# Attention with sinks and a two-layer product: chunk 0 masked in PSUM, its first product begun pair by pair, and chunk 1 moved ahead

## The chip, the core and the metric

The kernel runs on one NeuronCore of a Trainium2 chip. The core has five engines that run their own instruction queues: TensorE (PE, matrix products into PSUM), VectorE (DVE), ScalarE (ACT), GpSimd (POOL, which here issues the loads that also cast from float32 to bf16) and SyncE (SP, which here issues the other DMAs). They meet through semaphores. Sixteen DMA engines carry the transfers of all queues. The metric is the device time of one execution in microseconds (us); less is better. In the listings q0 is the DMA queue that POOL feeds, q1 the one that SP and ACT feed.

## The reference, cut to what matters

```python
batch, n_heads, seq, head_dim = (4, 8, 768, 64)
n_sink, window = (4, 64)
is_retrieval = [1, 0, 1, 0, 0, 0, 1, 0]
# attention, per batch and head
scores = (q @ k.T) / sqrt(head_dim)
causal = rel >= 0                                  # rel = query position - key position
keep   = causal & (key_pos < n_sink | (rel < window))
mask   = causal if is_retrieval[head] else keep
a      = softmax(where(mask, scores, -1e9))
x      = a @ v                                     # heads side by side: (3072, 512)
# two products with a leaky ReLU between
h   = x @ w_in                                     # 512 -> 2048
g   = maximum(0.01 * h, h)
out = g @ w_out                                    # 2048 -> 512, float32
```

Inputs and output are float32. The heads with full causal attention (0, 2, 6) are called retrieval heads below, the other five stream heads.

## The kernel before, in words

The 3072 tokens (4 batches of 768) are cut into eight chunks of 384 (`CH`); chunk n is half c of batch b, `divmod(n, 2)`. The schedule is written out by hand: the order of the Python calls is the order of the instructions on each engine, and the semaphores follow from it. Each chunk passes through these steps.

- **Loads** (`load`, `load_w`). POOL issues q, k and v in three transfers of 128 tokens each, and each weight in four quarters. At most eight of POOL's transfers are under way, because each waits for the eighth one before it. Chunk 0's k comes through SP into a float32 tile (`load_k0`).
- **Preparation.** q and k are transposed so that the head dimension lies on the partitions. `prep_first` (chunk 0) and `prep_pair` (chunks 1 and 2, one pair of heads at a time) use PE transposes into PSUM, followed by copies on DVE or ACT into `qts[n]` and `kt[b % 2]`. Chunks 3 to 7 use DMA transposes on SP (`prep_dma`), out of the buffers `kz` and `qb`. `zeros` and `zeros_k` clear the halves that must be zero. `v_shift` makes `vb`, the values moved by 64 tokens, with two DMAs on SP; `v_shift_pe` makes it for chunk 0 with products and copies.
- **Attention** (`Attention`). Each unit has a score part `qk` (products into a PSUM bank, an exponential on ACT into `at` or `ats`, a mask multiplication on DVE) and a value part `do_av`, which follows `LAG` slots later. The value parts of a head pair accumulate in one bank `po`; `finish` adds the sink's part, takes the reciprocal of the last column (`linv`) and writes the scaled rows `xs`. `x_t` transposes `xs` on PE and ACT copies it to `xts[n]`. From chunk 4 on this is a DMA transpose instead. `slots` cuts the whole into slots, so that other work can be merged between them.
- **Product 1** (`in_slots`): sixteen tiles of 128 rows of h, each four products into one bank (`ph`, at L497) and one leaky ReLU on ACT into `gs[n]` (L499).
- **Product 2** (`out_slots`): three token tiles, each sixteen products of 512 columns (L510), cut into five or six slots; then a DVE copy to `o` and a store on SP.

Eight PSUM banks are shared by tag: `ph`, `psS` and `po` have two each, `py` and `pt` one. `merge` puts one list of slots evenly among another.

The order at the start is chunk 0's preparation, its attention `a0`, eight tiles of its product 1 (`in0[0:8]`), then chunk 1's preparation pair by pair among further tiles and the first scores of chunk 1's attention `a1`, the rest of `a1` among the rest of `in0` and half of `out0`, and then chunk 1's product 1 merged with the rest of `out0`. Between them POOL issues, in this order: q and v of chunk 0, w_in quarter 0, two small masks, w_in quarters 1 and 2, k, q and v of chunk 1, w_in quarter 3, w_out, then chunks 2 and 3. `warm_up` and the extra transposes in `x_t` are products whose result nobody reads; they keep PE running while it waits. From chunk 2 on a loop merges product 1 of chunk n, product 2 of chunk n - 1 and the attention of chunk n + 1.

Of the kernel before, what the change touches and what calls it, by code (L numbers as in the profile page):

```python
# [11 lines left out]
FP32 = mybir.dt.float32  # L12
# [9 lines left out]
def kernel(  # L22
# [119 lines left out]

    def mask_causal():
        nc.gpsimd.memset(m_caus[:], 1.0)
        keep(m_caus[:], [[1, 128]], ALU.is_ge, 0, -1)

    def masks():
        nc.gpsimd.memset(m_w[:], 1.0)
        keep(m_w[:], [[-1, 64]], ALU.is_gt, 0, 1)
        keep(m_w[:], [[1, 64]], ALU.is_ge, 64, -1)  # L150

        nc.gpsimd.memset(m_h[:], 1.0)
        keep(m_h[:], [[-NS, H]], ALU.is_ge, 0, 1)
        keep(m_h[:], [[NS, H]], ALU.is_ge, NS - 1, -1)
# [8 lines left out]

    def late_constants():
# [3 lines left out]
        for h in range(H):  # L168
            if IS_RETR[h]:
                nc.vector.memset(m_h[:, h : h + 1], 0.0)  # L170
# [28 lines left out]
    def v_shift_pe():  # L199

        w = 7 * (D + 1)
        for t in range(2):
# [5 lines left out]
            if t == 0:  # L208
                nc.scalar.activation(out=vb[0][:, t, 1:H, :], in_=src, func=ACTF.Copy)
            else:  # L210
                nc.vector.tensor_copy(vb[0][:, t, 1:H, :], src)
# [8 lines left out]
    def prep_pair(n, p, tag="pt", eng=("v", "v", "v")):  # L220
# [20 lines left out]
        move(eng[2], qts[n][:, p, :], pt[:, 1, 0:3, :])  # L241

# [17 lines left out]
    def prep_first():  # L260
# [36 lines left out]

        k_rows(0, 0)
        k_rows(0, 1)
        shifts()  # L300
        k_rows(1, 0, True)
        k_rows(1, 1)
        for h in range(H):
            sink_keys(0, h // 2, h % 2)
# [9 lines left out]
    class Attention:  # L314
# [37 lines left out]
        def retr(self, h):  # L352
# [5 lines left out]
            for grp in groups:  # L358
                box = {}

                def qk(grp=grp, box=box):
                    s = self.score()
                    a = rot.tile([128, CH], BF16, name="at", tag="at", bufs=6)
                    off = 0
                    for j, (kj, lo) in enumerate(grp):
# [5 lines left out]
                        off += w  # L371
                    nc.scalar.activation(out=a[:, 0:off], in_=s[:, 0:off], func=ACTF.Exp, scale=SM)  # L372
                    if len(grp) == 2:
# [18 lines left out]
        def stream(self, h):  # L392
# [4 lines left out]
            def qk():  # L397
# [3 lines left out]
                for m in range(6):  # L401
# [4 lines left out]
                        skip_group_check=True)  # L406
                av_ = a[:, :, 0:4:3, :]
                nc.scalar.activation(  # L408
                    out=av_, in_=s[:, 0:CH].rearrange("p (j e f) -> p j e f", j=3, e=2),
                    func=ACTF.Exp, scale=SM)  # L410
                if c == 0:
# [34 lines left out]
        def x_t(self, p, xs, tag="pt"):  # L446
            pt = bank(tag, [128, 2, 4, 128], BF16)
            for j in range((6, 4, 6, 10)[p] if self.n == 0 else 0):
# [3 lines left out]
            nc.scalar.activation(out=xts[self.n][:, p, :], in_=pt[:, 0, 0:3, :], func=ACTF.Copy)  # L452

        def slots(self, extra=(), order=range(H), extra_at=None, LAG=2, XLAG=3, sink_after=None):

            extra = list(extra)
# [9 lines left out]
            r, box = [], {}  # L466
# [102 lines left out]
    for i in range(4):  # L569
        load_w("out", i)  # L570
# [94 lines left out]
```

## Time and profile before

| | |
|---|---|
| device time, median of 4 runs | 244.95 us (244.54 to 245.69) |
| the profiled execution | 244.54 us, its span 242.8 us |
| granted PE clock | 1.00 throughout |
| start of the first score, of product 1 | 9.74 us, 19.47 us |
| start of product 1 of chunk 1, of chunk 2 | 49.46 us, 81.41 us |
| product 1 (L497) | 492 matmuls recorded, 326 ns each |
| product 2 (L510, banks py) | 238 recorded, 371 ns each |
| loads by POOL (q0) | 13.24 MB as written, 74.4% of 16 engines |
| other DMA (q1) | 16.95 MB, 35.6% of 16 engines |

The span runs from the first to the last recorded instruction. A matmul's recorded length includes the time in the pipeline, so that lengths of neighbours overlap; the distance between two starts is what PE gives to one. The shares of the DMA queues are the time that their packets took, and those of two queues overlap. A row of the timeline gives the start, the length, the engine and line, the operation with target and source, how often it comes in a row, and in brackets how long the engine was idle before it and what released it.

### The profile page before, as it was taken

The page shows a single profiled execution, that of the slowest core. Times are in us where ns is not written, and L with a number is a line of the kernel's source. Part 1 is how long each engine was busy: PE and PEld are TensorE (multiplying, and loading weights), DVE is VectorE, ACT ScalarE, POOL GpSimd, SP SyncE. Part 2 cuts the span into 40 slices and gives each one's busy share as a digit, 9 for nine tenths or more (in the row PEclk, how much of TensorE's full clock was granted, in tenths as well). Part 3 has the DMA queues.
Part 4 walks back from the last instruction along what each step waited for, and adds up shares of the span by engine and source line. Part 5 has one row for each costly group of instructions (what it writes and reads, how often), then busy time and mean ns, then how long its engine had stood idle before and what let it go on. Part 6 is the DMA issues. An engine that isn't in the chain of part 4 may idle for free.

```text
span 242.8 us, 5110 instructions
## 1 busy us (share of the span) xinstructions
PE 228.9 (94%) x2028; PEld 138.7 (57%) x2056; DVE 90.5 (37%) x261; ACT 131.5 (54%) x285; POOL 78.3 (32%) x106
## 2 busy tenths in 40 slices
PE   7989889899999999899997999999999999999994
PEld 2765546556665667466544566566556665455553
DVE  6898422616465234334410343234411352111121
ACT  2776688433753698656445664466447764333300
POOL 7976832788109863384450000000000000000000
PEclk9999999999999999999999999999999999999999
DMA  9999999999999999999999932377220211111112
GB/s 162 143 180 166 178 233 196 154 182 134 156 155 209 199 130 147 161 174 142 199 140 179 170 99 62 90 152 140 76 62 0 63 32 59 46 43 43 44 45 86
DMA packets 112779, 30.54 MB, mean 126 GB/s; under 512 B 103540, under 2 KB 108916, under 8 KB 112756
## 3 DMA queue, kind: packets, MB, share of 16 engines
q0 software_dynamic: 76224, 13.24, 74.4%
q1 hardware_dynamic: 36432, 16.95, 35.6%
q8 instruction: 16, 0.26, 0.5%
q14 instruction: 7, 0.06, 0.1%
q10 hardware_dynamic: 100, 0.02, 0.1%
HBM read 27.28 MB, written 6.29 MB: 138 GB/s over the span
## 4 chain that ended last, share of the span: by engine, by line
PE 78%; DMA 8%; POOL 6%; ACT 3%; DVE 3%; issue 2%; POOLq 0%
PE ph L497 29%; PE py L510 20%; PE po L334 6%; PE pt L510 6%; PE psS L367 5%; DMA qb<-in_q_dram 4%; PE psS L510 4%; DMA xt<-xs 3%; PE ph L510 3%; PE psS L403 2%; POOL qb L93 2%; PE psS L347 2%; DVE o L515 1%; POOL kb L93 1%; POOL va L93 1%
## 5 line engine op out<-in xcount | busy, mean ns | idle before, releaser
L497 PE MATMUL ph<-xt,w_in_bf 128*128 128x384 bf16 x492 | 100.0, 326 | 1.5 <-DMA xt<-xs 1.4
L499 ACT ACTIVATE g<-ph 128x384 bf16<-128x384 f32 x123 | 60.5, 492 | 59.0 <-PE ph L497 58.3
L510 PE MATMUL py<-w_out_bf,g 128*128 128x512 bf16 (+1 forms) x238 | 63.4, 371 | 2.1 <-DVE o L515 0.6
L497 PEld LDWEIGHTS <-w_in_bf 128*128 128x128 bf16 x512 | 45.8, 97 | 29.5 <-issue 0.5
L510 PEld LDWEIGHTS <-g 128*128 128x128 bf16 x400 | 36.0, 97 | 28.9 <-issue 2.2
L372 ACT ACTIVATE at<-psS 128x384 bf16<-128x384 f32 x81 | 38.9, 491 | 12.7 <-PE psS L367 10.9
L93 POOL DMA_DIRECT2D qb<-in_q_dram x24 | 21.4, 902 | 21.7 <-DMA qt<-qb 10.6
L515 DVE COPY o<-py 128x512 f32<-128x512 f32 (+1 forms) x16 | 10.8, 674 | 45.3 <-PE py L510 45.0
L86 POOL DMA_DIRECT2D kz<-in_k_dram x30 | 22.5, 770 | 15.9 <-DMA kt<-kz 12.7
L367 PE MATMUL psS<-qt,kt 128*128 128x384 bf16 (+2 forms) x104 | 25.9, 290 | 1.3 <-ACT at L372 1.1
L93 POOL DMA_DIRECT2D va<-in_v_dram x24 | 21.2, 900 | 9.1 <-DMA w_in_bf<-in_moe_w_in_dram 3.1
L408 ACT ACTIVATE ats<-psS 128x384 bf16<-128x384 f32 x38 | 18.6, 493 | 5.2 <-PE psS L403 4.8
L334 PE MATMUL po<-va,at 128*128 128x65 bf16 x237 | 20.2, 194 | 0.3 <-DVE at L376 0.3
L334 PEld LDWEIGHTS <-at 128*128 128x128 bf16 x252 | 15.8, 98 | 7.4 <-DVE at L376 1.4
L440 DVE TENSOR_TENSOR xs<-po,linv 128x384 bf16<-128x384 f32 x30 | 16.7, 557 | 1.0
L378 DVE TENSOR_TENSOR at<-at,m_caus 128x128 bf16<-128x128 bf16 x24 | 5.4, 224 | 31.0 <-ACT at L372 31.0
L367 PEld LDWEIGHTS <-kt 128*128 128x128 bf16 x108 | 10.4, 98 | 10.4 <-issue 3.0
L510 PE MATMUL pt<-w_out_bf,g 128*128 128x512 bf16 x57 | 15.7, 379 | 0.4
L403 PEld LDWEIGHTS <-kt 128*128 128x128 bf16 x240 | 11.8, 98 | 5.5 <-issue 0.2
L334 PEld LDWEIGHTS <-ats 128*128 128x128 bf16 x240 | 11.6, 97 | 4.3 <-issue 0.8
L376 DVE TENSOR_TENSOR at<-at,m_caus 128x256 bf16<-128x256 bf16 x24 | 7.0, 292 | 16.1 <-ACT at L372 16.0
L403 PE MATMUL psS<-qt,kt 128*128 128x64 bf16 x228 | 12.8, 193 | 0.0
(115 smaller groups left out, 199.3 us busy)
## 6 DMA issues: line engine op xcount, KB each, us to landing
out_dram<-o SPq DMA_DIRECT2D x23, 256.0 KB, 3.0
qb<-in_q_dram POOLq DMA_DIRECT2D x24, 128.0 KB, 7.3
va<-in_v_dram POOLq DMA_DIRECT2D x24, 128.0 KB, 7.6
w_in_bf<-in_moe_w_in_dram POOLq DMA_DIRECT2D x4, 512.0 KB, 8.0
w_out_bf<-in_moe_w_out_dram POOLq DMA_DIRECT2D x4, 512.0 KB, 13.3
kz<-in_k_dram POOLq DMA_DIRECT2D x30, 64.0 KB, 7.9
vb<-va SPq DMA_DIRECT2D x8, 195.0 KB, 7.3
vb<-va SPq DMA_DIRECT2D x6, 130.0 KB, 5.9
```

The lines of the kernel that those rows point to most:

```text
L86: nc.gpsimd.dma_start(out=kz[n % 2][:, g, hh::2, D * hh : D * hh + D], in_=nat[nm][b, c, :, hh::2, g])
L93: nc.gpsimd.dma_start(out=o, in_=nat[nm][b, c, :, :, g])
L334: nc.tensor.matmul(o, lhsT=lhsT, rhs=rhs, start=first, stop=False, skip_group_check=True)
L367: nc.tensor.matmul(s[:, off : off + w], lhsT=kt[i][:, p, hh, 128 * kj : 128 * kj + 128], rhs=qts[n][:, p, lo:CH], start=(j == 0), stop=(j ...
L372: nc.scalar.activation(out=a[:, 0:off], in_=s[:, 0:off], func=ACTF.Exp, scale=SM)
L403: nc.tensor.matmul(s[:, 64 * m : 64 * m + 64], lhsT=kt[i][:, p, hh, k0 : k0 + 128], rhs=qts[n][:, p, 64 * m : 64 * m + 64], start=(m == 0) ...
L408: nc.scalar.activation(out=av_, in_=s[:, 0:CH].rearrange("p (j e f) -> p j e f", j=3, e=2), func=ACTF.Exp, scale=SM)
L440: nc.vector.tensor_tensor(xs[:], po[:, :, :, 0:D], linv.to_broadcast([128, 3, 2, D]), op=ALU.mult)
L497: nc.tensor.matmul(ph[:, 0:CH], lhsT=w_in_bf[:, g, 128 * t : 128 * t + 128], rhs=xts[n][:, g, :], start=(g == 0), stop=(g == KG - 1))
L499: nc.scalar.activation(out=gs[n][:, t, :], in_=ph[:, 0:CH], func=ACTF.Prelu, alpha=0.01)
L510: nc.tensor.matmul(py[n][:, 0 : c1 - c0], lhsT=gs[n][:, ng, 128 * tt : 128 * tt + 128], rhs=w_out_bf[:, ng, c0:c1], start=(ng == 0), stop= ...
L515: nc.vector.tensor_copy(o[:, 0 : c1 - c0], py[n][:, 0 : c1 - c0])
```

## The change

The masks of chunk 0 are no longer multiplied into the exponentials on DVE. Negative masks `n_caus` and `n_win0` (0 where a score is kept, -30000 where not) are added to the scores in PSUM by a product with the identity. `masks` builds them, `m_w` and `m_h` on DVE, in `prep_first`, ahead of the kt copies; POOL's masks go. The second of chunk 0's four kt copies moves from DVE to ACT, and one `vb` copy from ACT to DVE. DVE's clearing of `kt[0]` for chunk 1 moves into chunk 0's attention; that of `kz` moves to POOL.

The first four tiles of chunk 0's product 1 (`in_first`) are computed side by side in four banks, one head pair after another, between the `x_t` of the pairs. Then all of chunk 1 is prepared at once (`prep_two`, two head pairs in one bank, with larger copies). Chunk 1's k and q are loaded ahead of w_in quarter 1, and its v ahead of quarter 2. The value parts of chunk 1 follow their scores by ten slots at first, two at the end (`lag`), with thirteen `at` buffers. Product 1 of chunk 1 comes ahead of most of product 2 of chunk 0, whose first tile uses a bank of tag `psS`. `load(4)` and `prep_dma(3)` keep their places in the list of calls, while chunk 2's preparation comes later in it.

```diff
+    def negative(out, m):
+        nc.vector.tensor_scalar(out, m, NEG, -NEG, op0=ALU.mult, op1=ALU.add)
+
+    def masks():
+        with nc.allow_low_precision("one term of each sum is not zero"):
+            nc.vector.tensor_reduce(m_h[:], ident[:, 0 : NS * H].rearrange("p (h r) -> p h r", r=NS),
+                                    axis=mybir.AxisListType.X, op=ALU.add)
+        for h in range(H):
+            if IS_RETR[h]:
+                nc.vector.memset(m_h[:, h : h + 1], 0.0)
+        negative(n_caus[:], m_caus[:])
+        nc.vector.tensor_sub(m_w[:], m_caus[:, 64:128], m_caus[:, 0:64])
+        nc.vector.tensor_copy(n_win0[:, 0, :], n_caus[:, 0:64])
+        negative(n_win0[:, 1:], spread(m_w[:], 5, 64))
+        nc.vector.memset(n_win0[0:NS, 1, :], 0.0)
...
+    def prep_two(n, nm, half, tag, eng):
...
+        pt = bank(tag, [128, 2, 4, 128], BF16)
+        for e in range(2):
+            p = 2 * half + e
+            for g in range(3):
+                nc.tensor.transpose(pt[:, e, g, :], cast[nm, n][:, g, 2 * p : 2 * p + 2, :], ident[:])
...
+        if nm == "k":
+            for hh in range(2):
+                r = slice(64 * hh, 64 * hh + 64)
+                move(eng[hh], kt[b % 2][r, ps2, hh, CH * c : CH * c + CH], pt[r, :, 0:3, :])
+        else:
+            for e in range(2):
+                p2 = slice(2 * half + e, 2 * half + e + 1)
+                move(eng[e], qts[n][:, p2, :], pt[:, e : e + 1, 0:3, :])
...
+        masks()
         k_rows(0, 0)
-        k_rows(0, 1)
-        shifts()
+        k_rows(0, 1, True)
         k_rows(1, 0, True)
         k_rows(1, 1)
+        shifts()
...
-                    a = rot.tile([128, CH], BF16, name="at", tag="at", bufs=6)
+                    a = rot.tile([128, CH], BF16, name="at", tag="at", bufs=13)
...
+                    if n == 0:
+                        for o in (0,) if len(grp) == 1 else (0, 256):
+                            nc.tensor.matmul(s[:, o : o + 128], lhsT=ident[:], rhs=n_caus[:], start=False,
+                                             stop=True, skip_group_check=True)
...
+                if n == 0:
+                    nc.tensor.matmul(s[:, 0:CH], lhsT=ident[:], rhs=n_win0.rearrange("p m t -> p (m t)"),
+                                     start=False, stop=True, skip_group_check=True)
...
+    def in_first(n, tags):
+        phs = []
+        def step(g):
+            if g == 0:
+                phs.extend(in_bank(n, t, tag) for t, tag in enumerate(tags))
+            for t, ph in enumerate(phs):
+                in_part(n, t, ph, g)
+                if g == KG - 1:
+                    leaky(n, t, ph)
+        return [lambda g=g: step(g) for g in range(KG)]
...
     load_w("in", 0)
-    masks()
+    load(1, "kq")
     load_w("in", 1)
+    load(1, "v")
     load_w("in", 2)
-    load(1)
     load_w("in", 3)
...
+    for t in kz:
+        nc.gpsimd.memset(t[:, :, 0::2, D:], 0.0)
+        nc.gpsimd.memset(t[:, :, 1::2, 0:D], 0.0)
     prep_first()
-    a0 = Attention(0, ("psS", "ph"), po_tags=("po", "po", "py", "po"),
-                   x_tags=("pt", "ph", "psS", "pt")).slots(order=[0, 2, 1, 3, 4, 5, 6, 7], LAG=4, XLAG=3, sink_after={0, 2})
-    warm_up(12)
+    A0 = Attention(0, ("psS", "ph"), po_tags=("po", "po", "py", "po"))
+    a0 = A0.slots(order=[0, 2, 1, 3, 4, 5, 6, 7], lag=lambda t: 4, XLAG=None, sink_after={0, 2})
+    warm_up(8)
     run(a0[0:4])
-    late_constants()
-    run(a0[4:6])
     sink_values(0)
+    zeros(0, 1)
+    run(a0[4:6])
     v_shift_pe()
-    run(a0[6:])
-    zeros(0, 1)
-    nc.vector.memset(ksink[1][:], 0.0)
-    zeros(1, 0)
-    zeros_k(1)
-    zeros_k(0)
+    run(a0[6:15])
+    i0 = in_first(0, ("ph", "psS", "ph", "psS"))
+    A0.x_t(0, "pt", 4)
+    run(a0[15:])
+    A0.x_t(1, "po", 6)
+    run(i0[0:1])
+    A0.x_t(2, "pt")
+    run(i0[1:2])
+    A0.x_t(3, "py")
+    run(i0[2:4])
+    in0 = in_slots(0, ("ph",))
+    prep_two(1, "k", 0, "py", "vs")
+    prep_two(1, "k", 1, "pt", "vs")
+    prep_two(1, "q", 0, "py", "sv")
+    prep_two(1, "q", 1, "pt", "sv")
     load(2)
     load(3)
-    in0 = in_slots(0, ("ph", "psS"))
-    run(in0[0:8])
...
+    A1 = Attention(1, po_tags=("po", "po", "po", "pt"), x_tags=("py",))
+    a1 = A1.slots(order=[0, 2, 6, 1, 3, 4, 5, 7], lag=lambda t: max(2, 10 - t // 2))
+    run(a1[0:4])
     v_shift(1, nc.sync)
-    run(a1[3:6])
-    run(merge(in0[11:], a1[6:14]))
-    out0 = out_slots(0, ("py", "py", "py"))
-    run(merge(out0[0:8], a1[14:] + [lambda: None] * 6))
+    run(merge(in0[4:8], a1[4:10]), a1[10:14])
+    run(merge(in0[8:12], a1[14:20]))
+    out0 = out_slots(0, ("psS", "ph", "py"))
+    run(merge(in0[12:16] + out0[0:3], a1[20:]))
+    late_constants()
+    nc.vector.memset(ksink[1][:], 0.0)
+    zeros(1, 0)
     v_shift(2, nc.sync)
     load(4)
+    in1 = in_slots(1)
+    run(in1[0:12], merge(in1[12:], out0[3:5]))
     run(prep_dma(3))
-    x = merge(in_slots(1), out0[8:])
-    run(x[:8])
     a2 = [lambda j=j: prep_pair(2, j, ("pt", "psS")[j % 2]) for j in range(4)] + Attention(2).slots()
-    run(merge(x[8:] + out_slots(1, ("ph", "py", "ph")), a2))
+    run(merge(out0[5:] + out_slots(1, ("ph", "py", "ph")), a2))
```

## The prediction

> **What bounds the kernel now.** I read the page's rows by slice first, then the windows, then the timelines of the first 50 us engine by engine, then the waits of POOL and of the tile xt. TensorE (PE) has the work:
>
> ```profile
> PE 228.9 (94%) x2028; PEld 138.7 (57%) x2056; DVE 90.5 (37%) x261; ACT 131.5 (54%) x285; POOL 78.3 (32%) x106
> PEclk9999999999999999999999999999999999999999
> DMA  9999999999999999999999932377220211111112
> ```
>
> The clock is full throughout, and the DMA engines are taken until slice 23 (140 us). Busy PE overstates work, since a row's length contains the pipeline. I count work by the spacing of starts: a product-1 tile (four matmuls, L497) 0.65 us, an L510 matmul 0.216, an L367 score 0.162, a stream head's six L403 matmuls 0.18, a value matmul of L334 0.03, a transpose 0.055. The windows then divide the run:
>
> ```profile
> 24.92:49.46 24.54, 21.38 (x231) 13.61 (x232) 9.42 (x28) 16.62 (x39) 13.71 (x17) 1.00 1.78 190
> 49.46:81.41 31.95, 31.69 (x268) 19.09 (x272) 14.39 (x42) 14.77 (x32) 19.43 (x25) 1.00 1.70 169
> ```
>
> From 49.46 to 81.41 the work is 31.8 us (product 1 of chunk 1 10.4, 71 L510 matmuls 15.3, preparation and attention of chunk 2 6.1): nothing is lost. From 24.92 to 49.46 it is 19.3 us (24 transposes 1.3, eight product-1 tiles 5.2, attention of chunk 1 7.35, 25 L510 matmuls 5.4), so **5.2 us are lost**. Before 22 us PE waits on chains of copies. Hence only the start, the stage of chunk 1, and the few late waits on DMA can give anything.
>
> **1. Start of chunk 0.**
>
> ```profile
> 8.88 0.81 ACT L306 ACTIVATE qt<-po 128x768 bf16<-128x768 bf16 x1 [0.77 <-PE po L281]
> 9.74 0.32 PE L367 MATMUL ph<-qt,kt 128*128 128x384 bf16 x1
> 19.47 1.06 PE L497 MATMUL ph<-xt,w_in_bf 128*128 128x384 bf16 x4
> ```
>
> ScalarE (ACT) waits for the transposed q, copies it, and the first score follows at 9.74; product 1 starts at 19.47. The change puts the new masks on VectorE (DVE) after the cast that ends at 5.67 and ahead of the first kt copy. A reduction to 128x8 and a multiply-add do not occur in this trace. By neighbours (L438 0.19, L161 0.17, L165 0.31, the three L170 memsets 0.13) they make 1.3 us together; bounds 0.9 and 1.9. The kt copy could not start before 6.28 anyway, so it moves to 7.0 and lasts to 7.95 (L292, 0.97). The second kt copy goes to ACT. In the order of instructions it waits for DVE's copy out of the same bank, though the two read different partitions. *The row* nearest is an ACT copy of bank py that sat 1.74 us behind DVE's:
>
> ```profile
> 27.34 0.49 ACT L235 ACTIVATE qt<-py 128x384 bf16<-128x384 bf16 x1 [1.74 <-DVE kt L233]
> ```
>
> *The rule* is that of the Trainium skill, page "PSUM — Partial Sum Buffer", section "PSUM bank collisions raise a hardware error": access need be kept apart only by bank and 32-partition quadrant. Rows 0-63 and 64-127 are different quadrants, so by the rule ACT starts at 6.3 and the first score stays at 9.74. By the row ACT does 7.95 + 0.80 + 0.80 + 0.81 = 10.35, first score 10.4: **0.7 later**. I take the row, because the order names the wait; no run here shows the rule's case.
>
> DVE goes on in a line: kt copy after ACT's (9.55 to 10.5), shifts 0.25, ksink 0.76, second q half 0.56 (ends 12.1, was 10.89), sink values 0.7, two kt memsets moved here at 0.9 each, two vb copies 1.1: 15.8 us. In the old trace the first vb consumer waited too, at 14.32 for 0.66. The mask multiplications are gone (11 on DVE, about 2.7 us by starts), and PE takes them over: nine 128-column and five 384-column products, 1.3 us, beside DVE's line. One output pair costs 0.8 (linv and xs, 15.12 to 15.91), so xs are ready at 16.7, 17.5, 18.3, 19.1. Product 1 by pairs then starts with the first pair, and only its last quarter waits for the fourth: x_t(3) behind step 1 ends 19.9, its copy 20.65, step 3 ends **21.4**. Before, the same four tiles ended at 19.47 + 4 x 0.65 = 22.07. Part 1: **-0.7**.
>
> **2. Chunk 1 prepared at once.** Its k and q are now ahead of three weight quarters. By the trace's completions w_in 0 lands at 15.7, a 128-token load takes 0.95, a quarter 2.5: q lands at 21.4 (before 26.2), w_in 1 at 24, v 27, w_in 2 29, w_in 3 31. No product meets a missing weight (tile 4 needs w_in 1 near 27, tile 8 w_in 2 near 33). That removes this wait:
>
> ```profile
> 26.26 0.23 PE L228 MATMUL py<-ident,qb 128*128 128x128 bf16 x1 [0.59 <-DMA qb<-in_q_dram]
> ```
>
> In its place stands a chain: ACT finishes four g tiles (0.385 each by starts) at 22.75, kt of both halves 0.80 each to 24.35, q copy 0.49; first score 24.9. PE has 24 transposes, 1.3 us, in these 3.5: a **gap of 2.2**, with nothing beside it. Then ACT and two psS banks pace PE:
>
> ```profile
> 31.16 2.35 ACT L372 ACTIVATE at<-psS 128x384 bf16<-128x384 f32 x5
> 30.79 0.32 PE L367 MATMUL psS<-qt,kt 128*128 128x384 bf16 x1 [0.62 <-ACT at L372]
> ```
>
> Five exponentials take 2.35, 0.47 each. Followed one by one, fifteen of them (7.05) and the four g copies between (another 1.25 where they push in) last 8.3 us, beside 5.8 of PE work: 2.5 lost. The longer lag (ten slots) hides the masks; it does not add score banks. The stream heads stand among product-1 tiles, 0.2 lost. Work to the start of chunk 1's product 1 is 17.1 (7.8 + 7.35 + 1.95), so it starts at 24.9 + 17.1 + 2.7 = 44.7. Before, less the 16 L510 matmuls which now come later, 49.46 - 3.46 = 46.0. Parts 1 and 2: **-1.3**.
>
> **3. Product 1 of chunk 1 alone.** Thirteen tiles follow each other on two ph banks. A g copy begins 0.85 after its tile (20.37 to 21.22) and lasts 0.49; the bank is wanted after 1.30. That is 0.05 a tile, **+0.65** (bounds 0 and 1.0). DVE's moved constants and memsets (2.9 us) lie beside it.
>
> **4. What the reordering does to DMA.**
>
> ```profile
> 72.44 2.63 POOL L93 DMA_DIRECT2D qb<-in_q_dram  x3 [10.55 <-DMA qt<-qb]
> 101.50 0.32 PE L367 MATMUL psS<-qt,kt 128*128 128x384 bf16 x1
> 128.86 0.32 PE L497 MATMUL ph<-xt,w_in_bf 128*128 128x384 bf16 x1 [1.38 <-DMA xt<-xs]
> ```
>
> POOL idles 10.55 us because chunk 4's q needs the buffer that chunk 3's DMA transposes read. In the new order it waits for PE's transposes of chunk 2 instead, about 60 us, so loads 4 and 5 move some 10 us up and leave the transposes of chunks 4 and 5 and of xt less company. Two late waits hang on that: the one at 101.50 (q landed at 101.4; about 0.45 lost around it) and the 1.38. I take -0.4 and -1.2; bounds 0 and -1.8. Against it: SyncE (SP) issues chunk 0's first output ahead of chunk 3's transposes, and that output comes 10 us later. The transposes start near 58 instead of 51.94, their queue lands 4 us later, and so do the outputs behind them. The third output tile's buffer must have landed before DVE's copy at about 77 (77.41 before; landed 74.3). Behind that copy stand the last xs and PE's x_t. I take +0.3; bounds 0 and 3. Chunk 3's own operands (71.9 before, wanted at 81) keep 4 us. kz memsets on POOL lie behind w_out, whose queue is full to 42.4: nothing.
>
> **Sum** against the profiled execution: -1.3 + 0.65 - 1.6 + 0.3 = -1.95, 244.54 (span 242.8 and 1.7 around it) to 242.6. The median is 0.4 above the profiled run: **243.0**.
>
> **Rivals.** A change under 0.5% (1.2 us) can't be told from none here.
> - *The start is not late* (the rule holds, masks at 0.9) and the score stage loses 1.5 us rather than 2.7: 243.0 - 0.7 - 0.9 = 241.4. For it: DVE has 0.6 idle before 6.28. Against it: the named wait.
> - *No change*: chunk 3's later transposes eat the DMA gain (late waits as before, +1.6; the o wait 0.6 instead of 0.3): 243.0 + 1.6 + 0.3 = 244.9. For it: the DMA row is full until 140 us.
> - *Slower*, the gap of part 2: between 21.4 and 24.9 PE runs nothing but transposes. The Trainium skill ("TensorE: Matmul & The Clock Gate", the sections on PE-mode transpose and on why this matters) says that transposes don't count as activity, and that an idle gap over some 3 us returns the clock to half. The rows say 1.00 in every window, but none there has such a gap. By the rows it costs nothing more; by the rule PE is slow for two windows of the page's 3.4 us, in which it is loaded 5.8 parts of 8.3: 4.8 us of work becomes 9.6, which is 2.8 more than the 6.8 hold: 245.8. It decides once the stretch without matmuls passes 3.4 us.
>
> **How the numbers follow.** Forecast 0.40, early start 0.18, no change 0.18, slower 0.24. Faster: 0.32 of the first and all of the second, 0.50. Same: 0.08, 0.13 and 0.01, 0.22. Slower: 0.05 and 0.23, 0.28. Signs are mixed; the forecast's own range is 241.7 to 244.3. The whole range reaches into both tails: 240.8 to 246.6.
>
> **What would show it.** Right: first score near 10.4, four tiles done by 21.4, a PE gap of 2 us at chunk 1's transposes, product 1 of chunk 1 at 44.7, no POOL wait of 10 us near 62, no xt wait near 128. Wrong: clock below 1.00 after 22 us, DVE's o copy waiting for an output near 77, or a start near 9.7.

## The result and the profile after

| | before | changed |
|---|---|---|
| device time, median (lowest to highest) | 245.82 us (242.7 to 249.22, 57 runs) | 244.26 us (243.12 to 247.27, 36 runs) |
| ratio, 95% interval | | 0.9956 (0.9940 to 0.9972) |
| the profiled execution, its span | 244.54 us, 242.8 us | 245.89 us, 244.2 us |
| mean granted PE clock of that execution | 1.00 | 0.986 |

The change makes the kernel faster by 0.44% (0.28 to 0.60%), which is 1.1 us. The forecast was 1.95, and a median of 243.0. Ratios leave out disturbed runs; medians hold all of them.

The page of the changed kernel, its totals and two rows of its slices:

```profile
PE 231.2 (95%) x2024; PEld 139.4 (57%) x2050; DVE 86.8 (36%) x248; ACT 132.9 (54%) x285; POOL 80.0 (33%) x104
PEclk9999689999999999999999999999999999999999
DMA  9999999999999999999999622275210111111012
```

DVE has less to do (86.8 us against 90.5), since the mask multiplications of chunk 0 and the clearing of `kz` are gone from it. New is the dip to 6 and 8 in the clock row, at slices 5 and 6 (24 to 37 us). The windows show where it begins (length, then busy time of PE, PEld, DVE, ACT and POOL, the clock, the DMA share, GB/s):

```profile
24.00:26.00 2.00, 1.12 (x13) 0.85 (x13) 0.15 (x1) 1.91 (x4) 1.50 (x3) 0.97 1.56 205
26.00:28.00 2.00, 1.54 (x5) 0.37 (x4) 0.56 (x2) 1.81 (x5) 2.00 (x3) 0.50 1.22 199
28.00:30.00 2.00, 2.00 (x8) 1.07 (x8) 0.52 (x2) 1.03 (x3) 2.00 (x4) 0.50 1.24 212
...
32.00:34.00 2.00, 2.00 (x11) 1.03 (x10) 0.00 (x0) 1.47 (x5) 0.62 (x1) 0.82 1.24 206
```

PE stands at chunk 1's preparation, and when it resumes the clock is at half for about 6.8 us. The timeline of the changed kernel, by engine (start and length in us; in brackets the idle time before and who ended it):

```profile
7.87 0.81 ACT L324 ACTIVATE kt<-pt 64x768 bf16<-64x768 bf16 x1 [1.17 <-DVE kt L326]
10.25 0.32 PE L402 MATMUL ph<-qt,kt 128*128 128x384 bf16 x1 [0.75 <-ACT qt L341]
10.80 1.63 DVE L224 COPY ksink<-kt 64x4 bf16<-64x4 bf16 x5
13.09 0.38 PE L382 MATMUL ph<-qt,ksink 128*128 128x256 bf16 x2 [1.20 <-DVE qt L343]
...
24.66 0.49 PE L258 MATMUL py<-ident,qb 128*128 128x128 bf16 x6 [1.40 <-ACT kt L266]
25.87 0.80 PE L402 MATMUL psS<-qt,kt 128*128 128x384 bf16 x2
...
65.44 2.64 POOL L93 DMA_DIRECT2D qb<-in_q_dram  x3 [4.95 <-PE psS L234]
80.59 0.69 DVE L590 COPY o<-py 128x512 f32<-128x512 f32 x1 [0.72 <-DMA out_dram<-o]
130.20 0.32 PE L549 MATMUL ph<-xt,w_in_bf 128*128 128x384 bf16 x1 [0.55 <-DMA xt<-xs]
```

ACT does wait for DVE's copy out of the same bank (1.17), so the first score is at 10.25. The five `ksink` copies take 1.63 us where the old trace had 0.76 for the same five, and PE stands 1.20 for the sink scores. The POOL wait of 10.55 is now 4.95 and ends with PE; the `xt` wait is 0.55 where it was 1.38.

### The profile page after: what moved, and what is told of

Read it like the earlier page. It is cut to its first block, busy times and chain, and to the rows that moved or that the text cites. A ratio compares the mean times of both kernels' runs of the same rounds, so it can differ in the third digit from the quotient of the medians.

```text
span 244.2 us, 5083 instructions
## 1 busy us (share of the span) xinstructions
PE 231.2 (95%) x2024; PEld 139.4 (57%) x2050; DVE 86.8 (36%) x248; ACT 132.9 (54%) x285; POOL 80.0 (33%) x104
## 4 chain that ended last, share of the span: by engine, by line
PE 83%; DVE 7%; ACT 4%; DMA 3%; issue 2%; ACTq 0%
PE ph L549 31%; PE py L585 18%; PE po L369 7%; PE pt L585 6%; PE psS L402 5%; PE psS L585 5%; PE ph L585 4%; DMA xt<-xs 3%; PE psS L444 3%; PE psS L382 2%; ACT at L411 1%; DVE o L590 1%; ACT g L553 1%; DVE kt L326 1%; PE pt L499 1%
## 5 line engine op out<-in xcount | busy, mean ns | idle before, releaser
L549 PE MATMUL ph<-xt,w_in_bf 128*128 128x384 bf16 x504 | 103.6, 330 | 0.5 <-DMA xt<-xs 0.5
L553 ACT ACTIVATE g<-ph 128x384 bf16<-128x384 f32 x126 | 62.0, 492 | 56.0 <-PE ph L549 55.4
L549 PEld LDWEIGHTS <-w_in_bf 128*128 128x128 bf16 x512 | 46.6, 99 | 31.7 <-issue 2.8
L585 PE MATMUL py<-w_out_bf,g 128*128 128x512 bf16 (+1 forms) x211 | 55.7, 371 | 1.2
L402 PE MATMUL psS<-qt,kt 128*128 128x384 bf16 (+2 forms) x104 | 26.9, 304 | 0.8 <-ACT at L411 0.7
L590 DVE COPY o<-py 128x512 f32<-128x512 f32 (+1 forms) x14 | 9.4, 672 | 39.2 <-PE py L585 38.5
L369 PE MATMUL po<-va,at 128*128 128x65 bf16 x237 | 19.4, 194 | 0.3 <-DVE at L417 0.3
L402 PEld LDWEIGHTS <-kt 128*128 128x128 bf16 x108 | 10.5, 100 | 10.8 <-issue 3.4
L419 DVE TENSOR_TENSOR at<-at,m_caus 128x128 bf16<-128x128 bf16 x21 | 4.7, 223 | 29.9 <-ACT at L411 29.9
L585 PE MATMUL psS<-w_out_bf,g 128*128 128x512 bf16 (+1 forms) x61 | 12.9, 351 | 0.2
```

What stands on the lines that cost most here:

```text
L369: nc.tensor.matmul(o, lhsT=lhsT, rhs=rhs, start=first, stop=False, skip_group_check=True)
L402: nc.tensor.matmul(s[:, off : off + w], lhsT=kt[i][:, p, hh, 128 * kj : 128 * kj + 128], rhs=qts[n][:, p, lo:CH], start=(j == 0), stop=(j ...
L549: nc.tensor.matmul(ph[:, 0:CH], lhsT=w_in_bf[:, g, 128 * t : 128 * t + 128], rhs=xts[n][:, g, :], start=(g == 0), stop=(g == KG - 1))
L553: nc.scalar.activation(out=gs[n][:, t, :], in_=ph[:, 0:CH], func=ACTF.Prelu, alpha=0.01)
L585: nc.tensor.matmul(py[n][:, 0 : c1 - c0], lhsT=gs[n][:, ng, 128 * tt : 128 * tt + 128], rhs=w_out_bf[:, ng, c0:c1], start=(ng == 0), stop= ...
L590: nc.vector.tensor_copy(o[:, 0 : c1 - c0], py[n][:, 0 : c1 - c0])
```

## The experiments

Theory: the forecast missed a slower VectorE chain at the start and the clock at the stand of chunk 1's preparation. Main rivals: ScalarE and two score banks set the pace anyway, or the DMA engines give back whatever is won ahead of them. Each kernel is the changed one (or, named b, the one before) with the edit shown. Below, a run "at full clock" has a mean granted clock of 0.996 or more; one stretch at half lowers the mean to about 0.993, two to 0.986. A stretch is 3.4 us long by the windows of e_fill_mm, e_prep_early and e_xpe; the 6.8 above are two.

### 1. The stand at chunk 1's preparation

The changed kernel again:

> The changed kernel again, beside the next three. Theory (the PE gap at chunk 1's preparation lets the clock fall[...]): its runs spread over granted clocks 1.00, about 0.993 and about 0.986 of the whole, one or two windows of 3.4 us at half, and over 2 us of time; the mean is 0.4 to 0.8% below the kernel before. Rival (the clock has nothing to do with it, the sum of stage 2 is simply larger): runs at clock 1.00 are as long as the others.

Measured: 244.28 us (12 runs), ratio 0.9928 (0.9898 to 0.9957). Its profiled run, at clock 0.999, took 242.74 us, the least of the twelve (the median of its eight runs at full clock is 244.21). It shows what the half clock cost the other trace. Timeline, PE:

```profile
45.30 9.14 PE L549 MATMUL ph<-xt,w_in_bf 128*128 128x384 bf16 x52
```

This is product 1 of chunk 1, thirteen tiles. It starts at 45.30, as in the traces of c_after_b, e_fill_tr and e_banks; in the first trace of the changed kernel it starts at 47.74, with the first score of chunk 1 at 25.87 in both. So two half-clock stretches cost 2.44 us.

Then the stand was filled, with products and with transposes whose results nobody reads:

```diff
     prep_two(1, "k", 1, "pt", "vs")
+    fill = bank("po", [128, 512], FP32)                  # e_fill_mm
+    for _ in range(7):
+        nc.tensor.matmul(fill[:], lhsT=idle["s"][:, 0:128], rhs=idle["s"][:], start=True, stop=True)
+    fill = bank("po", [128, 2, 4, 128], BF16)            # e_fill_tr
+    for j in range(27):
+        nc.tensor.transpose(fill[:, 1, j % 4, :], ident[:], ident[:])
     prep_two(1, "q", 0, "py", "sv")
```

> Seven unread products of 512 columns (1.5 us) between the k and the q transposes of chunk 1, where PE stands idle for 1.4 us waiting for ACT. Theory: the clock stays at 1.00 in every run, the gap costs no more than its own 2 us, and the time is that of the changed kernel's runs at clock 1.00, 0.3 to 0.6% below its median, with little spread. Rival: no change of time, or 0.1 to 0.3 us longer, because the fill delays the q transposes.

> The same gap filled by 27 transposes of the identity (1.5 us) instead of products. If transposes do not count as activity for the clock, as the Trainium skill says on PE-mode transposes, the clock falls as often as in the changed kernel and nothing is gained. If they count, it stays at 1.00 and the time is that of the kernel filled with products.

Measured: products 243.82 us, ratio 0.9923 (0.9885 to 0.9961); transposes 243.56 us, ratio 0.9905 (0.9868 to 0.9942). 10 of 12 and 7 of 8 runs were at full clock, against 8 of 12 of the changed kernel beside them. Of these two traces that of the products has a half-clock stretch, but at the other stand of PE, around the 1.20 us wait for the sink scores that ends at 13.09. So has the trace of e_xpe (part 4), in which nothing is filled (clock 0.72, 0.50 and 0.93 in three windows of 2 us from 12 on); the middle one:

```profile
14.00:16.00 2.00, 2.00 (x13) 0.92 (x11) 1.80 (x3) 0.59 (x2) 1.14 (x3) 0.50 2.37 156
```

A run that is not at full clock need not have lost it at chunk 1's preparation. Ratios alone don't part these kernels from the changed one, whose interval overlaps both.

Chunk 1's k prepared ahead of the last steps of the first four tiles, with the copies mostly on DVE:

```diff
     A0.x_t(3, "py")
+    prep_two(1, "k", 0, "po", "vv")
+    prep_two(1, "k", 1, "pt", "vv")
     run(i0[2:4])
     in0 = in_slots(0, ("ph",))
-    prep_two(1, "k", 0, "py", "vs")
-    prep_two(1, "k", 1, "pt", "vs")
-    prep_two(1, "q", 0, "py", "sv")
-    prep_two(1, "q", 1, "pt", "sv")
+    prep_two(1, "q", 0, "py", "vv")
+    prep_two(1, "q", 1, "po", "vs")
```

> The k transposes of chunk 1 stand ahead of the last two steps of the first four tiles, their four copies and two of the four q copies on DVE, which is idle there. Theory: the gap of 2.1 us closes to under 0.5, the first score of chunk 1 comes at about 23.9 instead of 25.9, the clock stays at 1.00, and the kernel is 2 us faster than the changed one at clock 1.00, some 1.3 to 1.6% below the kernel before. Rival (ACT and the two score banks pace this stage whatever precedes it): the first score comes earlier, but less than 1 us of it remains at the start of chunk 1's product 1.

Measured: 243.8 us, ratio 0.9933 (0.9901 to 0.9965). The first score of chunk 1 comes at 24.28 instead of 25.87, but then PE waits 0.93 for an exponential, 5 of 12 runs lose the clock, and in the trace (with one half-clock stretch) product 1 of chunk 1 starts at 45.72. Its runs below full clock are not longer than the others (medians 243.75 and 243.96). The rival is partly right: the stand moves to the scores.

Last, dose and answer: both stands filled, the stand lengthened, and the changed kernel beside them on one chip.

```diff
+                if self.n == 0 and p == 2:               # e_fill_two, in sink(); and the 27 of e_fill_tr
+                    fill = bank("py", [128, 2, 4, 128], BF16)
+                    for j in range(18):
+                        nc.tensor.transpose(fill[:, 1, j % 4, :], ident[:], ident[:])

     prep_two(1, "k", 1, "pt", "vs")
+    junk = rot.tile([128, 768], BF16, name="junk", tag="junk", bufs=1)   # e_gap_more
+    for _ in range(2):
+        nc.scalar.activation(out=junk[:], in_=w_in_bf[:, 0, 0:768], func=ACTF.Copy)
     prep_two(1, "q", 0, "py", "sv")
```

> The changed kernel once more, as the measure for the two beside it. Expected: clock below 0.996 in about 4 to 6 of 10 runs, median near 244.2 us, ratio 0.993 to 0.996.

> The changed kernel with unread identity transposes at both places where TensorE stands still between 11 and 26 us: 18 ahead of the third sink product of chunk 0 and 27 at chunk 1's preparation. Theory (the half-clock stretches come from these two stands): clock at 0.996 or more in all runs but at most one, median 0.4 to 0.6 us below that of the changed kernel beside it, ratio near 0.990. Rival (the half-clock stretches come from elsewhere and the earlier counts were chance): below 0.996 in a third of the runs or more, median as the changed kernel's.

> The changed kernel with two unread copies of 128x768 on ScalarE (about 1.6 us) between chunk 1's k and q copies: TensorE's stand there is 1.6 us longer. Theory (the length of this stand is what costs the clock): below 0.996 in over 70% of the runs, and the median is 1.6 us of stand plus 0.5 to 1 us of clock above the changed kernel's: 246.3 to 246.8 us. Rival (the stand is covered or the clock does not depend on it): the clock as often full as in the changed kernel, and at most 1.6 us more: 244.8 to 245.8 us.

Measured: changed kernel 243.93 us, ratio 0.9965 (0.9936 to 0.9995); both filled 243.45 us, ratio 0.9936 (0.9906 to 0.9966); lengthened 246.26 us, ratio 1.0052 (1.0023 to 1.0082). The longer stand lost the clock in 12 of 12 runs, six of them with two stretches, and costs 2.3 us for 1.74 of stand. Its timeline, PE:

```profile
27.61 0.48 PE L402 MATMUL psS<-qt,kt 128*128 128x384 bf16 x2 [1.76 <-ACT qt L266]
```

The windows of the same run, with the clock in the third column from the right:

```profile
26.00:28.00 2.00, 0.39 (x2) 0.19 (x2) 0.39 (x2) 1.91 (x5) 1.76 (x3) 1.00 1.27 200
28.00:30.00 2.00, 1.39 (x6) 0.57 (x5) 0.40 (x2) 1.71 (x4) 2.00 (x4) 0.52 1.26 203
30.00:32.00 2.00, 2.00 (x8) 0.88 (x6) 0.45 (x2) 1.13 (x3) 2.00 (x3) 0.50 1.13 227
```

The score waits 1.76 for ACT's copy, and the clock drops behind it. Filling both stands proved nothing here, since the changed kernel beside it lost the clock in only 1 of 12 runs, as did the filled one. Over all runs:

| stand at chunk 1's preparation | runs | not at full clock |
|---|---|---|
| as in the changed kernel | 61 | 24 (19 of 37 in the result, 4 of 12, 1 of 12) |
| the same, with another edit (e_start, e_banks, e_xpe, e_chain, e_banks_sp) | 50 | 23 (6 of 12, 6 of 12, 3 of 8, 0 of 6, 8 of 12) |
| moved (e_prep_early) | 12 | 5 |
| filled (e_fill_mm, e_fill_tr, e_fill_two, c_comb) | 38 | 4 (2 of 12, 1 of 8, 1 of 12, 0 of 6) |
| filled, with edits further back (c_comb_x, c_comb_sp) | 18 | 13 (3 of 6, 10 of 12) |
| 1.74 us longer (e_gap_more) | 12 | 12 |
| the kernel before, runs beside the experiments | 131 | 26 |

The changed kernel's own share runs from 1 of 12 to 19 of 37, so only kernels run on the same chip can be compared. There the four filled ones lost the clock in 4 of 38 runs and the unfilled ones (c_after, c_after_b, e_xpe) in 8 of 32: that filling helps is likely and not shown. That a longer stand costs the clock is shown (12 of 12, against 1 of 12 beside it). Where the kernel before loses it, no trace shows: its own and those of b_qb3 and b_xpe are at full clock.

In the 37 runs of the result that have a clock on record, 15 had one stretch (median 244.32, against 243.65 at full clock) and four had two (mean 245.67): 0.5 us a run on average. The kernel before loses about 0.3 (26 of 131, some 1.5 us each), so that by this estimate the clock takes only about 0.2 us of the change's gain. Beside each other on two chips the two kernels lost it about as often (5 of 24 and 11 of 60). The clock explains a part of the spread, since the runs of the result at full clock alone reach from 243.12 to 244.59, and little of the shortfall.

### 2. The VectorE chain of chunk 0

Masks behind the first kt copy (e_start); sink unit two heads later and vb copies ahead of the kt memsets (e_chain):

```diff
-        masks()                                          # e_start
         k_rows(0, 0)
+        masks()
         k_rows(0, 1, True)

-    ... XLAG=None, sink_after={0, 2})                    # e_chain
+    ... XLAG=None, sink_after={0, 1, 2, 3})
     sink_values(0)
-    zeros(0, 1)
     run(a0[4:6])
     v_shift_pe()
+    zeros(0, 1)
```

> The changed kernel with its five mask steps on VectorE moved behind the first kt copy. Theory (my sum: ScalarE waits for VectorE's copy out of the same PSUM bank, so 1.3 us of masks ahead of that copy push the start back): ScalarE's first kt copy starts near 7.25 instead of 7.87, the first score near 9.7 instead of 10.25, and about 0.5 us comes off the total (ratio to the kernel before 0.2% lower than the changed kernel's 0.993). Rival (the VectorE chain behind it sets the end of chunk 0's attention: ksink copies, q half, zeros, vb copies): the first score is earlier, but the masks only move down in the same chain, so the last xs stays near 19.9 and the total does not change.

> The changed kernel with the sink unit of chunk 0 two heads later and the vb copies ahead of the two kt memsets on VectorE. Theory (the 1 us that chunk 0 ends later than my sum had it is the VectorE chain: five ksink copies at 1.63 us instead of 0.76, and the vb copies behind everything): PE's 1.2 us wait for the sink score at 13.09 goes, the vb wait goes, the xs come 0.8 to 1.0 us earlier, the four tiles end near 21.4 instead of 22.4, and 0.8 to 1.0 us comes off the total. Rival: ScalarE's exponentials on two score banks set the end of chunk 0's attention anyway, or the time is lost again at chunk 1's preparation: under 0.3 us off.

Measured: e_start 243.9 us, ratio 0.993 (0.9897 to 0.9964); e_chain 243.12 us, ratio 0.990 (0.9854 to 0.9945). Two lines of the timeline of e_start, VectorE and PE:

```profile
10.73 1.09 DVE L224 COPY ksink<-kt 64x4 bf16<-64x4 bf16 x5
44.67 9.14 PE L549 MATMUL ph<-xt,w_in_bf 128*128 128x384 bf16 x52
```

The same of e_chain:

```profile
12.48 0.56 DVE L343 COPY qt<-po 128x768 bf16<-128x768 bf16 x1
44.66 9.14 PE L549 MATMUL ph<-xt,w_in_bf 128*128 128x384 bf16 x52
```

Each edit alone brings product 1 of chunk 1 from 45.30 to 44.67, the 44.7 of the forecast. So VectorE's chain is what makes this start late. That the 0.6 us last to the end is likely and not shown: the intervals overlap that of the changed kernel, and in the trace of e_chain an output copy waits 2.10 at 79.19, so that chunk 1's last output is copied at 81.45 (81.42 in c_after). In e_start the first score is only at 10.15 (expected 9.7), because VectorE's first copy waited 0.92 for PE's transposes; what it won is the `ksink` copies, 1.09 instead of 1.63. In e_chain the q half is as late as in the changed kernel (12.48), but the last of the four tiles begins its last product at 21.62 instead of 22.26, and the 1.2 us sink wait is gone: two thirds of what was expected.

Why the five `ksink` copies take longer can be read from the traces. In the kernel before they stand beside POOL's masks, and POOL's next loads begin only about when they end:

```profile
9.54 0.76 DVE L218 COPY ksink<-kt 64x4 bf16<-64x4 bf16 x5
10.23 1.51 POOL L99 DMA_DIRECT2D w_in_bf<-in_moe_w_in_dram  x2
```

In the changed kernel POOL has no such masks and issues loads one after the other from 8.89 on. Here are one of these issues and the second of the five copies:

```profile
10.62 0.93 POOL L93 DMA_DIRECT2D kb<-in_k_dram  x1
10.88 0.67 DVE L224 COPY ksink<-kt 64x4 bf16<-64x4 bf16 x1
```

Both end at 11.55. Three of the five copies (667, 650 and 581 ns) last to the end of an issue; the other two (166 and 161 ns) lie near the start of one. In e_start only one is held up (552 ns). Over all traces 90 of 380 `ksink` copies take more than 240 ns, and each of the 90 ends within 0.04 us of the end of a load's issue on POOL. No run moved POOL's issues away, so this rests on the times alone.

### 3. Three PSUM tags for product 1 of chunk 1

```diff
-    in1 = in_slots(1)
+    in1 = in_slots(1, ("ph", "pt", "ph", "py"))
```

> The changed kernel with product 1 of chunk 1 on three PSUM tags (ph, pt, ph, py) instead of two ph banks. Theory (part 3 of my sum, 0.05 us a tile lost to two banks): its thirteen tiles go from 0.70 to 0.65 each, the stretch from 9.15 to about 8.5 us, and the total falls by 0.65 us. Rival: the leaky copies on ScalarE (0.49 each) and not the banks pace it, or the gain is given back at the following wait: tiles stay at 0.70, or the total is unchanged.

Measured: 244.45 us, ratio 0.9935 (0.9901 to 0.9969). The tiles follow each other by 0.65, as the forecast had it, and the thirteen take 8.44 instead of 8.98. The median shows no gain. The six runs at full clock fall into two groups, three at 242.6 to 242.8 and three at 244.5 to 245.2; the trace is of the longest of them, so that it shows how the gain can be lost, not that it always is. Timeline of e_banks:

```profile
79.54 0.69 DVE L590 COPY o<-py 128x512 f32<-128x512 f32 x1 [2.33 <-DMA out_dram<-o]
80.99 0.34 PE L499 MATMUL pt<-ident,xs 128*128 128x128 bf16 x3 [0.42 <-DVE xs L487]
129.45 0.32 PE L549 MATMUL ph<-xt,w_in_bf 128*128 128x384 bf16 x1 [1.86 <-DMA xt<-xs]
```

VectorE waits 2.33 for an output buffer, the xs stands behind it, and PE waits for the xs (0.42); then xt is 1.86 late. To see which wait decides, SyncE's issues of chunk 3's transposes were put ahead of product 1 of chunk 1:

```diff
+    run(prep_dma(3))
     run(in1[0:12], merge(in1[12:], out0[3:5]))
-    run(prep_dma(3))
```

> The changed kernel with three PSUM tags for product 1 of chunk 1, as in the run of the tags alone, and besides SyncE's issues of chunk 3's transposes ahead of this product 1 instead of behind the first output of chunk 0. Theory (what the tags won, 0.65 us, was lost because chunk 0's outputs land behind chunk 3's transposes: VectorE's output copy near 79 waits 2.33 us and the last xs stands behind it): that copy waits under 0.7 us, TensorE's 0.42 near 81 goes, and at full clock it is 0.5 us faster than the tags alone: near 243.2 us. Rival (the xt wait near 129 takes all that comes earlier): the copy's wait is short, but the xt wait stays at 1.5 us or more and the time as with the tags alone, 243.7 at full clock.

Measured: 244.65 us, ratio 0.9961 (0.9924 to 0.9998). The output wait only moved, to 73.67 (2.26 us). And two waits of the kernel before are back, on POOL and PE:

```profile
71.01 2.63 POOL L93 DMA_DIRECT2D qb<-in_q_dram  x3 [9.69 <-DMA qt<-qb]
128.53 0.32 PE L549 MATMUL ph<-xt,w_in_bf 128*128 128x384 bf16 x1 [1.48 <-DMA xt<-xs]
```

Both theory and rival missed that chunk 0's first output, moved behind the transposes, makes the next buffer late in its turn.

### 4. The late waits on DMA

A third q buffer in the kernel before takes POOL's wait away and nothing else:

```diff
-                cast[nm, n] = rot.tile([128, 3, H, D], BF16, name=f"{nm}b", tag=f"{nm}b", bufs=2)
+                cast[nm, n] = rot.tile([128, 3, H, D], BF16, name=f"{nm}b", tag=f"{nm}b", bufs=3 if nm == "q" else 2)
```

> The kernel before with a third buffer for the q loads, nothing else: GpSimd's 10.55 us wait at 72.44 has no cause any more. Theory (part 4 of my sum: this wait is what makes chunk 4's q and xt late): the 10.55 goes, the wait of the first score of chunk 4 near 101.5 and the 1.38 wait of xt near 128.9 shrink, and 0.8 to 1.6 us come off (ratio 0.993 to 0.997). Rival: the earlier loads take DMA time from chunk 3's transposes and outputs, another transfer is late instead, and the ratio is 1.000 within 0.002.

Measured: 244.73 us, ratio 0.9968 (0.993 to 1.0006). Timeline of b_qb3, POOL and PE:

```profile
65.06 0.88 POOL L93 DMA_DIRECT2D qb<-in_q_dram  x1 [0.80 <-PE ph L497]
130.05 0.32 PE L497 MATMUL ph<-xt,w_in_bf 128*128 128x384 bf16 x1 [1.64 <-DMA xt<-xs]
```

The 10.55 is 0.80, and in this trace xt is as late as before. With e_banks (POOL waits 0.90, xt 1.86) this shows that xt can be late without POOL's wait. It does not show that the wait costs nothing: the trace is of a run of 245.75 us, and the median of b_qb3's ten runs at full clock is 244.60, 0.87 below that of the kernel before beside it (245.47), as the theory had it; the interval of the ratio just includes no change. What goes with a late xt over the 16 traces in which xt of chunk 4 comes by DMA is the end of the last loads: in six of them POOL's last issue ends after 125.4 us, and five of these wait 0.9 to 1.9 for xt; of the other ten, none waits more than 0.55. That is an association, its limit was drawn afterwards (e_gap_more ends at 125.34 and waits 0.50), and e_fill_two is its exception (125.66, no wait).

So x of chunk 4 was taken off the DMA, in both kernels:

```diff
-            a = Attention(n + 1, x_dma=late).slots()
+            a = Attention(n + 1, x_dma=n + 1 > 4).slots()
```

> The changed kernel with x of chunk 4 transposed by twelve TensorE transposes (and copied by ScalarE) instead of four DMA transposes, so that no product of chunk 4 hangs on a DMA that shares the engines with the last loads. Theory (at full clock the whole gain of the change is this late wait: up to 65 us the change saves 0.7 and costs 0.65): the wait for xt near 127 to 130 can't occur, the twelve transposes cost about 0.7 us, and the median is within 0.4 us of the changed kernel's (ratio to before near 0.993). Rival (other DMAs are as late: outputs or chunk 5's k and q): another wait of more than 0.5 us appears between 100 and 145 us and the ratio is over 0.996.

> The kernel before with the same edit alone: x of chunk 4 transposed by TensorE. Theory (the gain of the change is the late xt wait and what stands around it): the 1.38 us wait goes for 0.7 us of transposes, so the kernel before gains 0.5 to 1.0 us by this edit alone (ratio 0.996 to 0.998), and the distance to the changed kernel with the same edit shrinks from 1.8 us to under 1. Rival (the gain of the change lies in its start and in chunk 1): no gain here (ratio 0.999 to 1.003), and the distance stays near 1.8 us.

Measured: the changed kernel with it 243.69 us, ratio 0.9928 (0.9901 to 0.9955); the kernel before with it 245.19 us, ratio 0.997 (0.9935 to 1.0005). At full clock the kernel before gains 0.95 by it (244.23, 8 runs, against 245.18, 18 runs), and the distance between the two kernels with it is 0.78 (243.45 and 244.23); without it, on two other chips, it was 1.3. That is what the theory expected; over all runs the interval includes no change, so it is not settled. In the traces the place is plain. One window of the kernel before:

```profile
100.00:132.00 32.00, 30.14 (x246) 17.57 (x248) 9.23 (x28) 17.02 (x37) 16.45 (x20) 1.00 1.97 170
```

The same window of the changed kernel (c_after):

```profile
100.00:132.00 32.00, 31.87 (x268) 18.68 (x266) 10.22 (x30) 18.35 (x40) 12.98 (x16) 1.00 1.81 167
```

PE is busy 1.73 us more of the same 32, and POOL has four transfers fewer left to issue there. The output copies on VectorE say the same. That of chunk 1's last tile starts at 81.44 in the kernel before and at 81.42 in c_after (81.99 in c_after_b): up to there the change has won nothing. That of chunk 3's first tile, behind the xt wait, in the kernel before:

```profile
136.26 0.69 DVE L515 COPY o<-py 128x512 f32<-128x512 f32 x1 [2.25 <-PE py L510]
```

In c_after (135.11 in c_after_b):

```profile
134.45 0.69 DVE L590 COPY o<-py 128x512 f32<-128x512 f32 x1 [2.25 <-PE py L585]
```

So in these traces the whole gain at full clock, 1.8 us in c_after, is won behind 81 us.

### 5. Combinations

c_comb has the edits of e_start, e_chain and e_fill_tr; c_comb_x those, the three tags and x of chunk 4 on TensorE; c_comb_sp those of c_comb, the three tags and SyncE's earlier transposes.

> The changed kernel with four of the earlier edits together: masks behind the first kt copy, sink unit two heads later, vb copies ahead of the kt memsets, and 27 unread transposes in the gap at chunk 1's preparation. Theory (start chain and clock are the two terms that my sum missed): the clock stays at 0.998 or more in nearly all runs, product 1 of chunk 1 starts near 44.0 instead of 45.30, and the ratio is 0.986 to 0.989. Rival (a DMA wall near 127 us: what is gained ahead of it comes back as a wait for xt): product 1 starts near 44.0 too, but the xt wait returns with 0.5 to 1.5 us and the ratio stays at 0.990 to 0.992.

> The same combination with, besides, three PSUM tags for product 1 of chunk 1 and x of chunk 4 transposed by TensorE. Theory (the DMA wall at xt is what made the three tags worth nothing): 1.3 us from the start, 0.65 from the tags, less 0.7 for the transposes; about 241.2 us at full clock and a ratio of 0.982 to 0.986, lower than the combination without it. Rival (something else behind it is as late): waits of over 0.5 us between 75 and 145 us, and a ratio of 0.988 or more.

> The combination (masks behind the first kt copy, sink unit later, vb copies earlier, transposes in the gap) with the three tags and with chunk 3's transposes issued ahead. Theory (start, tags and output wait add up): product 1 of chunk 1 starts at 44.0, its tiles take 0.65, no output copy waits over 0.7 us near 78, about 242.1 us at full clock and a ratio of 0.984 to 0.988. Rival (late xt near 127): the xt wait is 0.5 us or more and the ratio 0.989 to 0.992, no better than the combination without the two edits.

| | median | ratio | at full clock |
|---|---|---|---|
| c_comb | 242.75 us | 0.9898 (0.9854 to 0.9941) | 6 of 6 |
| c_comb_x | 244.98 us | 0.9890 (0.9831 to 0.9949) | 3 of 6, median 242.99 |
| c_comb_sp | 245.97 us | 1.0010 (0.9972 to 1.0048) | 2 of 12 |

c_comb has the lowest median of all, 2.4 us below the kernel before beside it; product 1 of chunk 1 starts at 44.02, and no xt wait returns. Its ratio lies between the ranges of theory and rival, and its interval overlaps that of the changed kernel, so that its lead over the changed kernel is likely and not shown. c_comb_x came out as its rival had it (0.9890, and a wait of over 2 us); c_comb_sp missed both theory and rival. The timeline of c_comb_sp, VectorE and then PE:

```profile
75.04 0.69 DVE L590 COPY o<-ph 128x512 f32<-128x512 f32 x1 [4.41 <-DMA out_dram<-o]
76.06 0.29 PE L369 MATMUL po<-va,ats 128*128 128x65 bf16 x2 [2.35 <-DVE ats L462]
```

Its windows there:

```profile
74.00:76.00 2.00, 0.00 (x0) 0.00 (x0) 0.96 (x3) 0.29 (x1) 2.00 (x4) 1.00 1.21 339
76.00:78.00 2.00, 1.94 (x13) 1.11 (x14) 1.66 (x6) 0.00 (x0) 2.00 (x3) 0.51 1.86 122
```

VectorE holds an output copy for 4.41 us, the masks that stand behind it hold PE for 2.35, and after that the clock is at half: here one wait for an output buffer cost its own length and then a stretch of clock. Ten of its 12 runs were not at full clock. In c_comb_x the output copy at 78.43 waits 2.39 and PE 0.48, much as in e_banks.

## Why the prediction was off

By its own steps, with c_after, its shortest run, as the trace at full clock:

| step | forecast | measured |
|---|---|---|
| masks on DVE, and the bank's order | first score 10.4 | 10.25 |
| four tiles done | 21.4 | 22.4 |
| first score of chunk 1 | 24.9 | 25.87 |
| parts 1 and 2: product 1 of chunk 1 starts (46.0 before) | 44.7 | 45.30 |
| part 3: thirteen tiles | +0.65 | +0.54 (8.98 against 8.44 in e_banks) |
| late waits (101.5 and xt) | -1.6 | -1.8 in c_after; xt 0.55 left in the first trace |
| wait for the output buffer | +0.3 | DVE 0.72 to 1.13, PE none |
| clock | 0 | 2.44 in the first trace, about 0.2 net over the runs, by estimate |

- **The step that failed** is the line "DVE goes on in a line: kt copy after ACT's (9.55 to 10.5), shifts 0.25, ksink 0.76, second q half 0.56 (ends 12.1, was 10.89)". The order was right and the durations were taken from the old trace, in which POOL's loads began only with the last of the `ksink` copies. With POOL's masks gone they stand beside all five, three copies last until an issue ends, and `ksink` took 1.63 instead of 0.76; the q half ended at 13.04, and all behind it came 0.6 to 1.0 later. At full clock the medians of the two kernels are 1.3 us apart (244.21 and 245.52 beside c_after, 243.84 and 245.16 beside c_after_b), 0.65 short of the 1.95. That is the size of this step, and e_start and e_chain each gave product 1 its forecast start back; that nothing else is missing from the total is not shown.
- **The clock** was costed "By the rows it costs nothing more", with 0.24 for the rival. The rows could not tell. The stretch without products is 3.3 us (22.6 to 25.87), just under the 3.4 of the rival. The clock did drop behind it in the first trace, and 24 of 61 runs were not at full clock, though not all need have lost it there. The all-or-nothing price was wrong: most runs pay nothing, the first trace 2.44 us.
- **The bank** was decided rightly for the row against the rule: ACT waited 1.17 for DVE.
- **Part 3** was right in size, but perhaps not a price of its own: e_banks takes it away, and its median gains nothing.
- **Part 4** was right in effect, and its cause stays open. It hung both late waits on POOL's 10.55; the traces of b_qb3 and e_banks have no such wait and a late xt, but at full clock b_qb3 is 0.87 us shorter than the kernel before. That c_after comes within 0.15 of the forecast 1.95 is partly luck: it is the shortest of twelve runs, and c_after_b's trace is 1.1 us below that of the kernel before.
- **The output buffer** was named with bounds 0 and 3. It costs PE nothing in the changed kernel, 0.42 in e_banks and 2.35 in c_comb_sp: the bound belonged to the edits around it.
- The rival of an early start did not occur (first score at 10.25), and its sum does not come out: 1.5 us lost rather than 2.7 is 1.2 less and not 0.9, which makes 241.1.
- The rival of no change is partly right: with the start won back, chunk 0's outputs and xt stand close behind.

## What to carry to other kernels

Where a change puts old operations beside new company, a duration from the old trace is itself an assumption: follow the one that a queue of others stands behind, see what the other engines will do in that stretch, and bound it. A stand of PE such as the 3.3 us here is a lottery for the clock; price it as its chance times a stretch, and compare chances only between kernels run side by side. And a gain ahead of the next late transfer is kept only as far as that transfer allows: look up when it lands before the gain is counted.

## What the runs showed that was not expected

- Whether transposes hold the clock stays open. The Trainium skill ("TensorE: Matmul & The Clock Gate", section "Part 4: PE-mode transpose") says that full clock doesn't engage for transposes. In the trace of e_fill_tr the 3.3 us stretch holds nothing else and the clock stays at 1.00, but in the unfilled traces of c_after and c_after_b it stays up too. On the same chips e_fill_tr and e_fill_two were at full clock in 18 of 20 runs, the changed kernel in 19 of 24. The longer stand of e_gap_more, filled with transposes, would tell; it was not run.
- The same five copies of 64x4 on VectorE took 0.76, 1.09 and 1.63 us in three orders, by how many of them were held up to the end of one of POOL's load issues. By these times, taking work off POOL (the masks) made work on VectorE slower.
- Moving one output behind six DMA transposes on SyncE's queue, together with three tags (c_comb_sp), turned the 1% of c_comb into nothing (ratio 1.0010).
